# One pool of five PSUM banks for the first products of two MLPs, on one Trainium2 core

## Chip, cores and metric

The kernel runs on one core of one Trainium2 chip. The metric is the device time of one execution in microseconds (us), as the median of several runs. Instructions are named with the line of the kernel that issues them (L683), and engines by short names: PE is TensorE (matmuls), PEld its weight loads, DVE is VectorE, ACT is ScalarE, POOL is GpSimd, SP issues most of the DMAs.

## What is computed

A long convolution (a Hyena filter) of 12480 tokens with 128 channels, gated by x, goes through two MLPs of 2048 inner features each, the first with an ELU, the second with a leaky ReLU of one slope per feature:

```python
h_filt = (np.maximum(pos_emb @ w1, 0.0) @ w2) * np.exp(-0.01 * pos)[:, None]
Uf = np.fft.rfft(x * v, n=2 * S, axis=1)
Hf = np.fft.rfft(h_filt, n=2 * S, axis=0)
x = x * np.fft.irfft(Uf * Hf, n=2 * S, axis=1)[:, :S]

h = x @ w_in                                   # first MLP, 128 -> 2048
g = np.where(h > 0.0, h, np.exp(np.minimum(h, 0.0)) - 1.0)
x = g @ w_out                                  # 2048 -> 128
h = x @ w_in2                                  # second MLP
g = np.maximum(h, 0.0) + alpha * np.minimum(h, 0.0)
out = g @ w_out2
```

## The kernel before

Up to some 280 us the kernel does the filter, the Fourier transforms (as matmuls) and the product of the spectra. The rest of the time belongs to the MLPs, and the change lies in them.

**Tiles and steps.** The tokens are cut into 26 tiles of columns: one of 392, twelve of 490, twelve of 485 (run as 486) and one of 388. Channels or features lie on the partitions. Each MLP takes a tile in 16 chunks of 128 features, so there are 416 steps, s = 16 t + c. In each step a chunk's first product h = x @ w_in is made in one PSUM bank, the activation is applied to it, and the second product adds it to the tile's output, which stays in a bank of its own for 16 steps. The second MLP runs 23 steps (`RAMP`) behind the first, since it needs the first one's finished tile: steps 0 to 22 are the first MLP's alone, then both run, and the last 23 steps are the second one's alone.

**Precision.** All operands are pairs of a rounded float32r value and its rest, `h` and `l` in the names. A product is therefore three matmuls (`mm3`, lines 638, 639 and 640): high x high, then high weights x low data, then low weights x high data. A step of both MLPs has four products, twelve matmuls on PE in this order: the first product of MLP 1 (tile `psh`, from `x1h`, `x1l`), the first product of MLP 2 (`psh`, from `x2h`, `x2l`), the second product of MLP 1 of three steps before (`pso`, from `g1h`, `g1l`), and that of MLP 2 (`pso`, from `g2h`, `g2l`).

**The activations.** For MLP 1, ACT makes exp(min(h, 0)) in two passes over the bank (L675, L676), or in one while MLP 1 is alone (L673, with a minimum on DVE at L682); DVE then takes the maximum with h (L683), which is the last reading of that bank. For MLP 2 all is on DVE: L701 (min, times alpha) and L706 (max, plus), the last reading of its bank. ACT rounds the result to the high half (L689 for `g1h`, L712 for `g2h`), and the low half is a subtraction (L661, `g1l` and `g2l`): one in four on DVE, the others on POOL, in other steps for the one MLP than for the other.

**The order.** The instructions of each engine stand in the order in which the loop at the end of the program writes them; no scheduler moves them. On DVE a step is: L701 and L706 of MLP 2, the low half of MLP 2 and that of MLP 1 of the step before (in the steps that are DVE's), and last L683 of MLP 1. An instruction that reuses a buffer waits for the last reader of what was in it.

**Other work beside the MLPs.** Once per tile the inverse transform (`inv2`, L539, 20 to 24 small matmuls into tile `psi`, read by DVE at L541) makes the next tile's input. From step 54 to 154 every fifth step has the transform of four high residues (`high_mm`): three matmuls of 512 columns, which DVE copies out (L587). In steps 10, 14, 18 and 22 there is a shorter one of a single matmul (L584), copied out by ACT.

**The eight PSUM banks** in the MLPs: two for `psi`, which `inv2` and `high_mm` share; two (`psh1`) for the first products of MLP 1 and two (`psh2`) for those of MLP 2; one each for the two outputs (`pso1`, `pso2`). While one MLP is alone, its first products take the four `psh` banks in turn (`tset`). So, while both run, the first product of MLP 1 in step s takes the bank that L683 of step s-2 has read last:

```python
    def tset(s, mlp):
        alone = s < RAMP if mlp == 1 else s >= NT * NFF - RAMP
        return 3 - mlp if alone and s % 2 else mlp
```

Of the kernel before, what the change touches and what calls it, by code (L numbers as in the profile page):

```python
# [9 lines left out]
F32 = mybir.dt.float32  # L10
# [4 lines left out]
PSUM = bass.MemoryType.PSUM  # L15
# [31 lines left out]
def kernel(ctx: ExitStack, tc: tile.TileContext, posT, w1b, w2b, sc2, xva, xT,  # L47
# [4 lines left out]
    def pool(name, bufs=1, **kw):  # L52
        return tc.tile_pool(name=name, bufs=bufs, reuse_waits="tile", **kw)
# [20 lines left out]
    def col(o, n):  # L74
        return ureg[:, o : o + n]
# [503 lines left out]
    def high_mm(i):  # L579
        y, n = hst.pop(i)  # L580
        z = col(512 * i if i < NFILL else 1024 + 512 * (i % 2), n * D)
        ps = pst.tile([128, 512], F32, name="psi")
        if i < NFILL:
            nc.tensor.matmul(ps[:, : n * D], w_sb, y, start=True, stop=True)  # L584
        else:
            mm3(ps, n * D, wf, yf, True, True)
        (nc.scalar.copy if i < NFILL else nc.vector.tensor_copy)(z.rearrange("q (f h c) -> q f h c", f=n, h=NCH),  # L587
                                                                 ps[:, : n * D].rearrange("q (h f c) -> q f h c", f=n, h=NCH))
        nc.sync.dma_start(zd[4 * i : 4 * i + n].rearrange("f q c -> q f c"), z.rearrange("q (f c) -> q f c", f=n))
# [28 lines left out]
    take(ctx.enter_context(pool("wp2")), "wi2l", "wo2h", "wo2l")  # L618
    gp = ctx.enter_context(pool("gp", 2, side="right"))
    pp.close()  # L620
    pst = ctx.enter_context(pool("pst", 2, space=PSUM))
    psm = ctx.enter_context(pool("psm", 2, space=PSUM))

    LAG = 3
    LAG_ALONE = 5
# [9 lines left out]
    def mm3(ps, w, a, b, start, stop):  # L635
        ah, al = a
        bh, bl = b
        nc.tensor.matmul(ps[:, :w], ah, bh[:, :w], start=start, stop=False)  # L638
        nc.tensor.matmul(ps[:, :w], ah, bl[:, :w], start=False, stop=False)  # L639
        nc.tensor.matmul(ps[:, :w], al, bh[:, :w], start=False, stop=stop)  # L640

    def wc(nm, c):
        return (wh[nm][0][:, c, :], wh[nm][1][:, c, :])
# [4 lines that stand above are left out]
# [4 lines left out]
    def h1_mm(s):  # L652
        t, c = divmod(s, NFF)
        hi, lo, w = x1[t]
        ps = psm.tile([128, 512], F32, name=f"psh{tset(s, 1)}")
        mm3(ps, w, wc("wi1", c), (hi, lo), True, True)
        st1[s] = [ps, w]

# [78 lines left out]
    def h2_mm(s):  # L737
        t, c = divmod(s, NFF)
        hi, lo, w = x2[t]
        ps = psm.tile([128, 512], F32, name=f"psh{tset(s, 2)}")  # L740
        mm3(ps, w, wc("wi2", c), (hi, lo), True, True)
        st2[s] = [ps, w]

# [29 lines left out]
    for i, x in enumerate(FILL):  # L773
        at(x, high_mm, i)
    for i in range(NFILL, (NF + 3) // 4):
        for d, fn in ((-1, high_load), (1, high_add), (2, high_split), (4, high_mm)):
            at(HS + 5 * i + d, fn, i)
# [10 lines left out]
    for s in range(-1, TOT + RAMP + LAG_ALONE + 1):  # L788
        if s >= 0:
            if s < TOT:  # L790
                h1_mm(s)
            s2 = s - RAMP
            if 0 <= s2 < TOT:
                h2_mm(s2)
# [129 lines left out]
```

## Time and profile before

| | us |
|---|---|
| median of 3 runs | 1480.73 (1479.01 to 1482.35) |
| span of the profiled execution, first to last instruction | 1475.1 |
| median less span | 5.6 |
| PE busy | 1415.1 (96%) |
| DVE busy | 1280.5 (87%) |
| ACT busy | 1076.3 (73%) |
| POOL busy | 1019.4 (69%) |

The page gives no other time of the profiled execution than its span. What lies around the span, before the first and after the last instruction, is taken from the median of the runs. Busy times are unions of the intervals that the profiler gives. A matmul is listed from its start to its modelled end, and the next one starts before that end, so PE's busy time isn't its time at its peak: distances from start to start tell more. In a list of waits, a row says which engine's instruction (line and tile) sat idle for which instruction of another engine: the sum in us, how often, and the longest. A weight load waits first where a matmul waits, since it stands right ahead of it.

### The profile page before, as it was taken

To read this page: it belongs to the slowest core of one execution; us is meant where nothing else is said; L and a number is where in the kernel's file an instruction comes from. 1 tells how busy PE (TensorE), PEld (TensorE's weight loads), DVE (VectorE), ACT (ScalarE), POOL (GpSimd) and SP (SyncE) were. 2 spreads that over 40 slices of the span, in tenths; PEclk is the share of its full clock that TensorE was granted. 3 is DMA by queue.
4 is the path that set the end of the run, shared out by engine and by line. 5 is a ranking of instruction groups with operands and counts; after the bars stand their busy time and mean duration, and the time that the engine had idled before them with its cause. 6 is when DMAs were issued, how large, how long until landed. Compare 5 with 4: busy or idle time off the path is not lost.

```text
span 1475.1 us, 26820 instructions
## 1 busy us (share of the span) xinstructions
PE 1415.1 (96%) x9935; PEld 1200.8 (81%) x9935; DVE 1280.5 (87%) x1812; ACT 1076.3 (73%) x2009; POOL 1019.4 (69%) x935
## 2 busy tenths in 40 slices
PE   7988778899999999999999999999999999999998
PEld 6878676888888878888888888888888888888887
DVE  5689986798888888888889999998999899889998
ACT  3445442478877787788878788888888787888884
POOL 4668975456778887888756676666666666766667
PEclk9999999999999999999999999999999999999999
DMA  8786898540131212212003200000000000000000
GB/s 258 235 267 174 225 276 210 197 132 18 38 89 51 89 60 68 89 51 78 31 25 127 82 18 26 25 25 25 8 18 25 25 25 8 18 25 22 7 8 13
DMA packets 70215, 117.64 MB, mean 80 GB/s; under 512 B 8806, under 2 KB 41258, under 8 KB 68920
## 3 DMA queue, kind: packets, MB, share of 16 engines
q1 hardware_dynamic: 65716, 104.49, 23.2%
q0 software_dynamic: 1296, 7.86, 1.6%
q10 hardware_dynamic: 3072, 3.57, 0.7%
q8 instruction: 78, 1.28, 0.4%
q14 instruction: 53, 0.43, 0.1%
HBM read 82.38 MB, written 32.80 MB: 78 GB/s over the span
## 4 chain that ended last, share of the span: by engine, by line
PE 64%; DVE 9%; ACT 5%; issue 3%; POOL 1%; DMA 1%; SPq 0%; POOLq 0%; ACTq 0%; DVEq 0%
PE psh L638 11%; PE psh L640 10%; PE psh L639 10%; PE pso L639 10%; PE pso L638 10%; PE pso L640 10%; PE psi L539 3%; DVE ureg L683 2%; DVE g1l L661 1%; DVE ureg L701 1%; ACT ureg L676 1%; DVE g2l L661 1%; ACT ureg L675 1%; DVE ureg L706 1%; ACT g2h L712 1%
## 5 line engine op out<-in xcount | busy, mean ns | idle before, releaser
L661 POOL TENSOR_TENSOR g2l<-ureg,g2h 128x490 fp32r<-128x490 f32 (+3 forms) x315 | 373.1, 1185 | 131.7 <-ACT g2h L712 62.4
L661 POOL TENSOR_TENSOR g1l<-ureg,g1h 128x486 fp32r<-128x486 f32 (+3 forms) x313 | 346.6, 1108 | 164.2 <-ACT g1h L689 160.8
L701 DVE TENSOR_SCALAR ureg<-psh,al_sb 128x486 f32<-128x486 f32 (+3 forms) x416 | 295.9, 711 | 80.0 <-PE psh L640 75.7
L675 ACT ACTIVATE ureg<-psh 128x490 f32<-128x490 f32 (+2 forms) x393 | 225.5, 574 | 112.9 <-PE psh L640 97.3
L706 DVE SCALAR_TENSOR_TENSOR ureg<-psh,ureg 128x486 f32<-128x486 f32 (+3 forms) x416 | 274.1, 659 | 14.3
L683 DVE SCALAR_TENSOR_TENSOR ureg<-ureg,psh 128x486 f32<-128x486 f32 (+3 forms) x416 | 268.2, 645 | 4.5 <-ACT ureg L676 3.2
L689 ACT CAST g1h<-ureg 128x490 fp32r<-128x490 f32 (+3 forms) x405 | 240.3, 593 | 16.0 <-DVE ureg L683 13.5
L676 ACT ACTIVATE ureg<-ureg 128x490 f32<-128x490 f32 (+2 forms) x393 | 239.7, 610 | 12.4
L712 ACT CAST g2h<-ureg 128x490 fp32r<-128x490 f32 (+3 forms) x404 | 234.6, 581 | 8.4 <-DVE ureg L706 6.8
L638 PE MATMUL psh<-x1h,wi1h 128*128 128x486 f32 (+3 forms) x416 | 170.2, 409 | 9.4 <-DVE ureg L683 6.9
L639 PE MATMUL psh<-x1l,wi1h 128*128 128x486 f32 (+3 forms) x416 | 158.7, 382 | 0.0
L640 PE MATMUL psh<-x1h,wi1l 128*128 128x486 f32 (+3 forms) x416 | 158.7, 381 | 0.0
L638 PE MATMUL psh<-x2h,wi2h 128*128 128x486 f32 (+3 forms) x416 | 158.7, 381 | 0.0
L639 PE MATMUL psh<-x2l,wi2h 128*128 128x486 f32 (+3 forms) x416 | 158.6, 381 | 0.0
L640 PE MATMUL psh<-x2h,wi2l 128*128 128x486 f32 (+3 forms) x416 | 158.3, 381 | 0.0
L638 PE MATMUL pso<-g1h,wo1h 128*128 128x490 f32 (+3 forms) x405 | 154.8, 382 | 1.5 <-ACT ureg L731 1.5
L639 PE MATMUL pso<-g2l,wo2h 128*128 128x490 f32 (+3 forms) x404 | 154.3, 382 | 0.7 <-POOL g2l L661 0.7
L640 PE MATMUL pso<-g1h,wo1l 128*128 128x490 f32 (+3 forms) x405 | 154.8, 382 | 0.0
L639 PE MATMUL pso<-g1l,wo1h 128*128 128x490 f32 (+3 forms) x405 | 154.6, 382 | 0.0
L640 PE MATMUL pso<-g2h,wo2l 128*128 128x490 f32 (+3 forms) x404 | 154.0, 381 | 0.0
L638 PE MATMUL pso<-g2h,wo2h 128*128 128x490 f32 (+3 forms) x404 | 153.8, 381 | 0.0
L661 DVE TENSOR_TENSOR g1l<-ureg,g1h 128x490 fp32r<-128x490 f32 (+3 forms) x104 | 124.7, 1199 | 19.3 <-ACT g1h L689 8.8
(167 smaller groups left out, 2531.9 us busy)
## 6 DMA issues: line engine op xcount, KB each, us to landing
ureg<-yd SPq DMA_DIRECT2D x50, 256.0 KB
yd<-rreg SPq DMA_DIRECT2D x22, 512.0 KB
rreg<-in_gmat_dram SPq DMA_DIRECT2D x24, 384.0 KB
ureg<-in_finv_dram SPq DMA_DIRECT2D x23, 379.0 KB
ureg<-zd SPq DMA_DIRECT2D x4, 1584.0 KB
x<-in_xva_dram SPq DMA_DIRECT2D x32, 196.0 KB
v<-in_xva_dram SPq DMA_DIRECT2D x32, 196.0 KB
zd<-ureg SPq DMA_DIRECT2D x24, 256.0 KB
```

The costliest lines, as they stand in the source:

```text
L539: nc.tensor.matmul(ps[w_, a * ni : (a + 1) * ni], z_sb[:, c * P + p0 + a, w_], fv[:, a, c, :ni], start=(c == 0), stop=(c == 1))
L638: nc.tensor.matmul(ps[:, :w], ah, bh[:, :w], start=start, stop=False)
L639: nc.tensor.matmul(ps[:, :w], ah, bl[:, :w], start=False, stop=False)
L640: nc.tensor.matmul(ps[:, :w], al, bh[:, :w], start=False, stop=stop)
L661: eng.tensor_tensor(lo[:, :w], e[:, :w], hi[:, :w], ALU.subtract)
L675: nc.scalar.activation(e[:, :w], ps[:, :w], AF.Relu, scale=-1.0)
L676: nc.scalar.activation(e[:, :w], e[:, :w], AF.Exp, scale=-1.0)
L683: nc.vector.scalar_tensor_tensor(e[:, :w], e[:, :w], -1.0, ps[:, :w], op0=ALU.add, op1=ALU.max)
L689: nc.scalar.copy(hi[:, :w], e[:, :w])
L701: nc.vector.tensor_scalar(e[:, :w], ps[:, :w], 0.0, al_sb[:, c : c + 1], op0=ALU.min, op1=ALU.mult)
L706: nc.vector.scalar_tensor_tensor(e[:, :w], ps[:, :w], 0.0, e[:, :w], op0=ALU.max, op1=ALU.add)
L712: nc.scalar.copy(hi[:, :w], e[:, :w])
```

## The change

The pool `pst` has one bank instead of two, for the inverse transform alone. The pool `psm` has five banks under one name, `psh`, beside the two for the outputs. The first products of both MLPs and the high residues' transform take their bank from those five, through `h_bank`. `tset` stays for the buffers in SBUF.

```diff
@@ high_mm
-        ps = pst.tile([128, 512], F32, name="psi")
+        ps = h_bank()
@@ pools
-    pst = ctx.enter_context(pool("pst", 2, space=PSUM))
-    psm = ctx.enter_context(pool("psm", 2, space=PSUM))
+    pst = ctx.enter_context(pool("pst", 1, space=PSUM))
+    psm = ctx.enter_context(pool("psm", 5, space=PSUM))
+
+    def h_bank():
+        return psm.tile([128, 512], F32, name="psh")
@@ h1_mm
-        ps = psm.tile([128, 512], F32, name=f"psh{tset(s, 1)}")
+        ps = h_bank()
@@ h2_mm
-        ps = psm.tile([128, 512], F32, name=f"psh{tset(s, 2)}")
+        ps = h_bank()
```

Each engine has the same instructions in the same order as before (lines behind 621 are numbered three higher). What differs are the banks and the waits. The pool hands out the bank that was let go longest ago, in the order of the program. In a step of both MLPs, where L706 stands ahead of L683, the first product of MLP 1 gets the bank that L683 of step s-3 read last, and the first product of MLP 2 the one that L706 of step s-2 read last. Behind a `high_mm`, for two steps, MLP 1 gets a bank let go by L706 of step s-2 and MLP 2 one let go by L683 of step s-2.

On PE, one step of both MLPs in the long stretch behind the high residues (x1h, x1l and x2h, x2l are the two MLPs' inputs, wi1, wi2 and wo1, wo2 the weights; DVE_49 is DVE's semaphore, Pool_49 POOL's, Activation_49 ACT's). Before:

```order
L638 MATMUL psh1_9269<-x1h_9100,wi1h_2996 128x486 [waits DVE_49]
L639 MATMUL psh1_9269<-x1l_9101,wi1h_2996 128x486
L640 MATMUL psh1_9269<-x1h_9100,wi1l_2997 128x486
L638 MATMUL psh2_9273<-x2h_8850,wi2h_3000 128x490
L639 MATMUL psh2_9273<-x2l_8851,wi2h_3000 128x490
L640 MATMUL psh2_9273<-x2h_8850,wi2l_3228 128x490
L638 MATMUL pso1_8879<-g1h_9225,wo1h_2998 128x490 [waits Activation_49]
```

And with the change:

```order
L641 MATMUL psh_9269<-x1h_9100,wi1h_2996 128x486 [waits DVE_49]
L642 MATMUL psh_9269<-x1l_9101,wi1h_2996 128x486
L643 MATMUL psh_9269<-x1h_9100,wi1l_2997 128x486
L641 MATMUL psh_9273<-x2h_8850,wi2h_3000 128x490 [waits DVE_49]
L642 MATMUL psh_9273<-x2l_8851,wi2h_3000 128x490
L643 MATMUL psh_9273<-x2h_8850,wi2l_3228 128x490
L641 MATMUL pso1_8879<-g1h_9225,wo1h_2998 128x490 [waits Activation_49]
```

The banks of the two MLPs are of one pool now, and the first product of MLP 2 has a wait for DVE of its own; before, the wait of the product ahead of it covered it.

On PE, behind a transform of high residues (tile read: yh, yl; weights: wh, wl), before:

```order
L638 MATMUL psi_5309<-yh_3244,wh_3242 128x512 [waits PE_49,Activation_49]
L639 MATMUL psi_5309<-yl_3245,wh_3242 128x512 [waits Pool_49]
L640 MATMUL psi_5309<-yh_3244,wl_3243 128x512
L638 MATMUL psh1_5317<-x1h_5159,wi1h_2996 128x490 [waits DVE_49]
L639 MATMUL psh1_5317<-x1l_5160,wi1h_2996 128x490
L640 MATMUL psh1_5317<-x1h_5159,wi1l_2997 128x490
L638 MATMUL psh2_5321<-x2h_4895,wi2h_3000 128x490
```

And with the change:

```order
L641 MATMUL psh_5309<-yh_3244,wh_3242 128x512 [waits DVE_49,Activation_49]
L642 MATMUL psh_5309<-yl_3245,wh_3242 128x512 [waits Pool_49]
L643 MATMUL psh_5309<-yh_3244,wl_3243 128x512
L641 MATMUL psh_5317<-x1h_5159,wi1h_2996 128x490 [waits DVE_49]
L642 MATMUL psh_5317<-x1l_5160,wi1h_2996 128x490
L643 MATMUL psh_5317<-x1h_5159,wi1l_2997 128x490
L641 MATMUL psh_5321<-x2h_4895,wi2h_3000 128x490 [waits DVE_49]
```

The transform's product takes one of the five banks and waits for DVE to have let go of it, where it waited for a bank of `psi`.

## Rows read from the trace of the kernel before

**Rows 1.** The page: span, busy time by engine, the chain that ended last.

```profile
span 1475.1 us, 26820 instructions
...
PE 1415.1 (96%) x9935; PEld 1200.8 (81%) x9935; DVE 1280.5 (87%) x1812; ACT 1076.3 (73%) x2009; POOL 1019.4 (69%) x935
...
PE 64%; DVE 9%; ACT 5%; issue 3%; POOL 1%; DMA 1%; SPq 0%; POOLq 0%; ACTq 0%; DVEq 0%
```

**Rows 2.** Windows: stretch, its us, busy PE, PEld, DVE, ACT, POOL, granted clock, DMA.

```profile
500.00:600.00 100.00, 98.13 (x497) 81.21 (x496) 85.90 (x126) 80.19 (x149) 81.58 (x67) 1.00 0.22 66
1000.00:1100.00 100.00, 99.61 (x507) 82.75 (x506) 90.11 (x128) 82.32 (x153) 66.36 (x60) 1.00 0.06 19
```

**Rows 3.** Waits of weight loads, 280:315, 315:402, 402:690, 690:1400, 1400:1475: us, times, longest.

```profile
PEld psh L638 <- DVE ureg L683: 5.1, 3, 3.3
...
PEld psh L638 <- DVE ureg L683: 5.0, 9, 1.5
...
PEld psh L638 <- DVE ureg L683: 6.7, 15, 1.0
...
PEld psh L638 <- DVE ureg L683: 19.6, 49, 0.6
...
PEld psh L638 <- DVE ureg L683: 1.2, 4, 0.4
```

**Rows 4.** Timeline, 900 to 906 us: start, duration, engine, instruction [idle before].

```profile
900.27 0.67 DVE L706 SCALAR_TENSOR_TENSOR ureg<-psh,ureg 128x490 f32<-128x490 f32 x1
...
901.87 0.65 DVE L683 SCALAR_TENSOR_TENSOR ureg<-ureg,psh 128x486 f32<-128x486 f32 x1
...
902.28 0.39 PE L640 MATMUL pso<-g2h,wo2l 128*128 128x490 f32 x1
...
902.57 0.19 PEld L638 LDWEIGHTS psh<-x1h,wi1h 128*128 128x128 f32 x1 [0.33 <-DVE ureg L683]
902.58 0.49 PE L638 MATMUL psh<-x1h,wi1h 128*128 128x486 f32 x1
...
902.90 0.38 PE L639 MATMUL psh<-x1l,wi1h 128*128 128x486 f32 x1
...
903.34 0.39 PE L638 MATMUL psh<-x2h,wi2h 128*128 128x490 f32 x1
...
905.12 0.39 PE L640 MATMUL pso<-g2h,wo2l 128*128 128x490 f32 x1
905.12 0.19 PEld L638 LDWEIGHTS psh<-x1h,wi1h 128*128 128x128 f32 x1
...
905.34 0.38 PE L638 MATMUL psh<-x1h,wi1h 128*128 128x486 f32 x1
```

**Rows 5.** Timeline of the first steps of the MLPs, around 288 and 320 us.

```profile
288.30 0.50 ACT L673 ACTIVATE ureg<-psh 128x392 f32<-128x392 f32 x1 [3.42 <-POOL ureg L571]
...
319.02 0.49 PE L638 MATMUL psh<-x1h,wi1h 128*128 128x490 f32 x1 [1.13 <-DVE ureg L683]
...
320.00 0.58 ACT L675 ACTIVATE ureg<-psh 128x490 f32<-128x490 f32 x1
```

**Rows 6.** Waits of DVE, 315:402, 402:690 and 690:1400 us.

```profile
DVE ureg L701 <- PE psh L640: 5.9, 11, 0.8
...
DVE ureg L701 <- PE psh L640: 20.9, 34, 1.0
...
DVE ureg L701 <- PE psh L640: 46.8, 87, 0.8
```

**Rows 7.** Timeline, 569 to 571 us.

```profile
569.47 1.06 POOL L661 TENSOR_TENSOR g1l<-ureg,g1h 128x490 fp32r<-128x490 f32 x1
...
570.61 0.46 PE L639 MATMUL pso<-g1l,wo1h 128*128 128x490 f32 x1
```

**Rows 8.** Tiles g1l and g2l, DVE's part: count, ns min/median/max, first and last start.

```profile
L661 DVE TENSOR_TENSOR g1l<-ureg,g1h x104: 557/1305/1506, 290.2 to 1434.5; 128x490 fp32r<-128x490 f32 x48, 128x486 fp32r<-128x486 f32 x48, 128x392 fp32r<-128x392 f32 x4, 128x388 fp32r<-128x388 f32 x4
...
L661 DVE TENSOR_TENSOR g2l<-ureg,g2h x100: 654/1138/1739, 327.5 to 1450.8; 128x490 fp32r<-128x490 f32 x48, 128x486 fp32r<-128x486 f32 x48, 128x392 fp32r<-128x392 f32 x4
```

## The prediction

> **What bounds the kernel now.** The page comes first: in a span of 1475.1 us TensorE is busy 96%, and the chain that ended last lies 64% on it [rows 1]. Then the busy time by stretches: between 500 and 600 us PE is busy 98.13 of 100 us, between 1000 and 1100 us 99.61, at a granted clock of 1.00 (its higher level) in both [rows 2]. Those numbers hide what is lost, because a matmul's modelled end overlaps the next start. What counts is the distance from start to start.
>
> The timeline shows it [rows 4]. Undisturbed, matmuls of 486 to 490 columns follow at 0.22 us: 905.12 to 905.34, with the weights of 905.34 loaded from 905.12 on. At 902.58 this breaks. The first product of the first MLP (L638, psh from x1h) needs a PSUM bank that DVE's L683 of two steps before has just let go: L683 starts at 901.87 and takes 0.65, so it ends at 902.52, and the weight load goes at 902.57 after 0.33 us of idleness. From 902.28 to 902.90 lie two distances, 0.62 instead of 0.44: 0.18 us are lost. So **a stall costs PE its listed weight-load wait less 0.15 us** (0.33 against 0.18).
>
> The waits of the weight loads by stretch [rows 3] give the sum of what this bank wait takes, at that 0.15 per stall:
> - 280 to 315 us (first MLP alone): 5.1 − 3 x 0.15 = 4.65
> - 315 to 402: 5.0 − 9 x 0.15 = 3.65
> - 402 to 690 (the high residues are done here): 6.7 − 15 x 0.15 = 4.45
> - 690 to 1400: 19.6 − 49 x 0.15 = 12.25
> - 1400 to the end: 1.2 − 4 x 0.15 = 0.6
>
> Together 25.6 us, 1.7% of the time. Is the next engine close behind? DVE waits for PE's products (L701 for L640) 5.9, 20.9 and 46.8 us in the three middle stretches [rows 6], 73.6 us in all, against 20.35 us lost by PE in the same ones. DVE is the nearest rival, but has 3.6 times what it needs.
>
> **The change part by part.** No instruction is added, removed or put elsewhere; only banks, and with them waits, change.
>
> *First product of the first MLP.* With two banks of its own it waits for L683 of step s−2, the last thing that DVE does in that step. From five banks, handed out in the order in which they were let go, it gets one that L683 of step s−3 released. In the stall shown, that bank was free a whole step earlier (a step is twelve distances of 0.22, 2.7 us), while the longest wait in 690 to 1400 us is 0.6. So this wait goes.
>
> *First product of the second MLP.* It now carries a wait of its own, for L706 of step s−2; behind it on PE stand eight more products of the step; DVE's L701 needs the first two of them, and the next step's products, which ACT's L675 needs, queue behind all eight. In the timeline that L706 ends at 900.94 and the product starts at 903.34 [rows 4], 2.4 us later: never late. A wait that is already fulfilled could still break the pulling ahead of weights; the row at 905.34 says no, since that product carried such a wait too and lost nothing. I take 0; the other end, the 0.10 of the late second distance (902.58 to 902.90 instead of 0.22) times 393, is excluded by that row.
>
> *The high residues' transform* takes one of the five banks every fifth step, and DVE's copy gives it back in the same step. In the two steps behind it the banks shift: the first MLP gets one released by L706, the second MLP one released by L683 of two steps before. That is the old wait, but three products (0.66 us) further on. The longest wait in 402 to 690 us is 1.0, a loss of 0.85, so at most some 0.2 of one stall is left. In the ramp ACT gives that bank back; it is let go about as early as DVE's. Nothing.
>
> *One bank for the inverse transform.* It is used once in 16 steps, over 40 us apart, and its reader follows within the step: 0.
>
> *What of the 25.6 is on the path.* 280 to 315: PE waits, but so does everyone: ACT starts its second exponential at 288.30 after 3.42 us of waiting for POOL [rows 5], and the ramp then runs at the pace of ACT and DVE. Taken 0, bounds 0 and 4.65. 315 to 402: the longest wait, 1.5 us before 319.02, stands in front of an ACT that starts the next L675 only at 320.00 [rows 5], so I count half of its 1.35: 3.65 − 0.7 = 2.95, bounds 2.3 (without that wait) and 3.65. 402 to 690: 4.45 less some 0.45 for the shifted banks and tight low halves (first rival) = 4.0, bounds 2.2 (half) and 4.45. 690 to 1400: 12.25 in full, since DVE has 46.8 us to spare there; the lower bound is 8.2, two thirds, as if every third stall only changed its cause. Behind 1400 DVE paces the end: 0, bounds 0 and 0.6. **Sum 2.95 + 4.0 + 12.25 = 19.2 us**, bounds 12.7 and 25.6.
>
> The profile gives the span, 1475.1; the median of the three runs, 1480.7, is 5.6 more, which lies around the span and doesn't change. So the span should be 1455.9, and the time **1461.5 us**.
>
> **The rivals.**
> - *Half the gain.* With PE earlier by up to 0.4 us, the next thing to be late is POOL's low half of g1, which the second product's L639 needs. For it: at 570.61 that product starts 0.08 us after POOL's 569.47 + 1.06 [rows 7], and POOL is busy 81.58 of 100 us in that stretch. Against it: POOL is busy only 66.36 in the longest one [rows 2]. If it gave back the 4.0 of 402 to 690 and half of the 12.25, 9.1 would remain: 1471.6.
> - *No change.* The loss only moves, because the end is set by DVE's total, and PE's stalls merely show it; or the pool hands the first MLP a bank of step s−2 as before. Against both: DVE's 73.6 us of waiting, and the order in which five banks come round. 1480.7.
> - *Slower: DVE's low halves stretch.* A quarter of the low halves of either MLP run on DVE, 104 and 100 of them, and one of g2 takes anything from 0.65 to 1.74 us; the medians are 1.31 and 1.14 [rows 8]. If PE's new rhythm laid each of them over a POOL operation, DVE would become the bound. The point from which this decides: the 73.6 us of slack spread over 204 operations are 0.36 us each, so their mean has to rise from about 1.2 to over 1.56 before anything is lost against now. At 1.6 it costs 0.4 x 204 − 73.6 = 8 us: 1488.7. It would take nearly the longest of them as the rule, so it is unlikely. The Trainium skill has the mechanism: "SBUF — State Buffer", section "Who interferes with whom", says that a DVE instruction with two SBUF inputs contends with a GpSimd instruction that reads SBUF. The trace agrees so far as one takes up to 2.7 times the shortest, at widths that differ by a quarter; how often the two would meet after the change it can't show.
>
> **How the numbers follow.** Forecast 0.78, half the gain 0.12, no change 0.06, slower 0.04. A measurement of this kernel can tell about 0.2%, 3 us, from no change. The first two are faster: 0.90; same 0.06; slower 0.04. The range runs from 1457 (nearly the whole 25.6) to 1470, past the lower bound of my sum (1480.7 − 12.7 = 1468.0) and up to the half-gain case; what lies outside is the better end of the ramp, that rival and the two below it, about 2 in 10.
>
> **What would show each step right or wrong.** Right: in 690 to 1400 us the weight loads' waits for DVE's release of psh fall from 49 to a handful, the first product is followed after 0.22 everywhere, DVE's wait for L640 shrinks by 10 to 15 us, and the stretch becomes 12 us shorter. The ramp up to 315 us keeps its length within 2 us. Half the gain: L639 on pso waits for POOL's g1l in dozens of places. Slower: DVE's L661 has a median near 1.6 and L701 no longer waits for PE. I am wrong if the bank waits are gone and the span isn't shorter by at least 11 us, or if the second MLP's product now waits.

## The result

The changed kernel takes 1459.24 us (median of 4 runs, 1457.69 to 1460.95), the kernel before beside it 1480.81 (4 runs, 1479.01 to 1482.35): a ratio of 0.9855, 95% interval 0.9841 to 0.9869. It is faster by 21.6 us. Forecast were 1461.5 and a range of 1457 to 1470. Medians and ratios in this text are of fast runs: one run of 7820 us (e1_third_mlp1) and one of 2286 us (r_after, at a granted clock of 0.556) are left out.

In the changed kernel the lines lie three further down: L641, L642 and L643 are the matmuls L638, L639 and L640, L686 is DVE's L683, L704 its L701, L664 the low halves of L661.

The page after, its span, busy times and chain, beside [rows 1]:

```profile
span 1458.0 us, 26810 instructions
...
PE 1401.9 (96%) x9935; PEld 1208.7 (83%) x9935; DVE 1278.4 (88%) x1812; ACT 1073.8 (74%) x2009; POOL 1019.6 (70%) x935
...
PE 77%; DVE 2%; DMA 1%; POOL 1%; issue 0%; ACT 0%; SPq 0%; POOLq 0%; DVEq 0%; ACTq 0%
```

PE's share of the span is 96% before and after, and says nothing. The chain does: 64% of it lay on PE, 9% on DVE and 5% on ACT; now it is 77, 2 and 0%. The windows after (stretch, its us, busy PE, PEld, DVE, ACT, POOL, granted clock, DMA), beside [rows 2]:

```profile
500.00:600.00 100.00, 98.36 (x503) 82.66 (x502) 87.06 (x127) 80.42 (x148) 84.16 (x69) 1.00 0.21 66
...
1000.00:1100.00 100.00, 100.00 (x517) 85.25 (x516) 91.93 (x130) 82.90 (x154) 66.91 (x61) 1.00 0.06 19
```

Between 1000 and 1100 us PE starts 517 matmuls where it started 507, and DVE is busier in the same 100 us because the same work comes in less time. The weight loads' waits after, in 402 to 687 and 687 to 1383 us (steps 54 to 150 and 150 to 400, as 402 to 690 and 690 to 1400 before), all of them, beside [rows 3]:

```profile
PEld psi L539 <- issue: 2.1, 6, 0.3
PEld pso L641 <- ACT ureg L734: 2.0, 1, 2.0
PEld pso L642 <- POOL g1l L664: 0.6, 3, 0.2
PEld pso L641 <- ACT ureg L758: 0.5, 1, 0.5
...
PEld psi L539 <- issue: 4.1, 12, 0.4
PEld psi L539 <- PE pso L642: 1.4, 4, 0.3
```

No weight load waits for DVE's release of a `psh` bank any more: 15 and 49 waits are 0 and 0, and nothing of their kind stands in their place (POOL's g1l: 3 waits, 0.6 us; the 2.0 us for L734 stood there before as 1.9 us for L731). The timeline shows it at the step of [rows 4], which now lies at 895:

```profile
891.65 0.65 DVE L686 SCALAR_TENSOR_TENSOR ureg<-ureg,psh 128x486 f32<-128x486 f32 x1
...
894.59 0.65 DVE L686 SCALAR_TENSOR_TENSOR ureg<-ureg,psh 128x486 f32<-128x486 f32 x1
...
894.97 0.39 PE L643 MATMUL pso<-g2h,wo2l 128*128 128x490 f32 x1
894.98 0.19 PEld L641 LDWEIGHTS psh<-x1h,wi1h 128*128 128x128 f32 x1
...
895.20 0.38 PE L641 MATMUL psh<-x1h,wi1h 128*128 128x486 f32 x1
895.20 0.19 PEld L642 LDWEIGHTS psh<-x1l,wi1h 128*128 128x128 f32 x1
895.41 0.39 PE L642 MATMUL psh<-x1l,wi1h 128*128 128x486 f32 x1
```

DVE is no earlier against PE than it was: its L686 of two steps before runs from 894.59 to 895.24. But the product takes the bank that the L686 before that one let go at 892.30, 2.9 us earlier, so its weights are pulled ahead at 894.98 while the late L686 still runs, and the matmuls follow at 0.23, 0.21.

What PE no longer waits for, DVE no longer has to spare. Its waits after, in 319 to 402, 402 to 687 and 687 to 1383 us, beside [rows 6]:

```profile
DVE ureg L704 <- PE psh L643: 2.6, 6, 0.7
...
DVE ureg L704 <- PE psh L643: 14.7, 29, 0.9
...
DVE ureg L704 <- PE psh L643: 34.7, 86, 0.8
```

They went from 73.6 to 52.0 us, 21.6 less. To place the gain I cut the MLPs by the starts of the first MLP's 416 first products, the last part ending with the last matmul:

| steps | before, us | after | gain | taken in the prediction |
|---|---|---|---|---|
| 0 to 23 | 32.68 | 33.69 | −1.01 | 0 |
| 23 to 54 | 86.21 | 82.43 | 3.78 | 2.95 |
| 54 to 150 | 288.94 | 285.12 | 3.82 | 4.0 |
| 150 to 400 | 709.18 | 696.35 | 12.83 | 12.25 |
| 400 to the last matmul | 71.82 | 71.33 | 0.50 | 0 |
| together | 1188.83 | 1168.92 | 19.9 | 19.2 |

### The profile page after: what moved, and what is told of

It reads as the page before. It is cut to its first block, busy times and chain, and to the rows that moved or that the text cites. A ratio compares the mean times of both kernels' runs of the same rounds, so it can differ in the third digit from the quotient of the medians.

```text
span 1458.0 us, 26810 instructions
## 1 busy us (share of the span) xinstructions
PE 1401.9 (96%) x9935; PEld 1208.7 (83%) x9935; DVE 1278.4 (88%) x1812; ACT 1073.8 (74%) x2009; POOL 1019.6 (70%) x935
## 4 chain that ended last, share of the span: by engine, by line
PE 77%; DVE 2%; DMA 1%; POOL 1%; issue 0%; ACT 0%; SPq 0%; POOLq 0%; DVEq 0%; ACTq 0%
PE psh L641 13%; PE psh L642 12%; PE psh L643 12%; PE pso L642 12%; PE pso L643 12%; PE pso L641 12%; PE psi L539 3%; DMA ureg<-yd 1%; DMA spreg<-in_wo_dram 0%; DVE ureg L704 0%; POOL ureg L571 0%; PE psh L584 0%; DVE wo1l L139 0%; DVE ureg L709 0%; SPq L402 0%
## 5 line engine op out<-in xcount | busy, mean ns | idle before, releaser
L664 POOL TENSOR_TENSOR g1l<-ureg,g1h 128x486 fp32r<-128x486 f32 (+3 forms) x313 | 346.6, 1107 | 163.3 <-ACT g1h L692 160.1
L664 POOL TENSOR_TENSOR g2l<-ureg,g2h 128x490 fp32r<-128x490 f32 (+3 forms) x315 | 373.5, 1186 | 110.5 <-ACT g2h L715 43.0
L704 DVE TENSOR_SCALAR ureg<-psh,al_sb 128x486 f32<-128x486 f32 (+3 forms) x416 | 295.9, 711 | 56.7 <-PE psh L643 53.4
L709 DVE SCALAR_TENSOR_TENSOR ureg<-psh,ureg 128x486 f32<-128x486 f32 (+3 forms) x416 | 274.1, 659 | 14.3
L686 DVE SCALAR_TENSOR_TENSOR ureg<-ureg,psh 128x486 f32<-128x486 f32 (+3 forms) x416 | 268.3, 645 | 4.7 <-ACT ureg L679 3.7
L641 PE MATMUL psh<-x1h,wi1h 128*128 128x486 f32 (+3 forms) x416 | 162.6, 391 | 3.6 <-DVE ureg L686 2.6
L643 PE MATMUL psh<-x1h,wi1l 128*128 128x486 f32 (+3 forms) x416 | 158.7, 381 | 0.0
L642 PE MATMUL psh<-x1l,wi1h 128*128 128x486 f32 (+3 forms) x416 | 158.5, 381 | 0.0
L641 PE MATMUL psh<-x2h,wi2h 128*128 128x486 f32 (+3 forms) x416 | 158.5, 381 | 0.0
L642 PE MATMUL psh<-x2l,wi2h 128*128 128x486 f32 (+3 forms) x416 | 158.4, 381 | 0.0
L643 PE MATMUL psh<-x2h,wi2l 128*128 128x486 f32 (+3 forms) x416 | 158.2, 380 | 0.0
L641 PE MATMUL pso<-g1h,wo1h 128*128 128x490 f32 (+3 forms) x405 | 155.1, 383 | 3.1 <-ACT ureg L734 1.6
L642 PE MATMUL pso<-g1l,wo1h 128*128 128x490 f32 (+3 forms) x405 | 155.0, 383 | 0.0
L643 PE MATMUL pso<-g1h,wo1l 128*128 128x490 f32 (+3 forms) x405 | 154.9, 383 | 0.0
L642 PE MATMUL pso<-g2l,wo2h 128*128 128x490 f32 (+3 forms) x404 | 154.3, 382 | 0.6 <-POOL g2l L664 0.6
L641 PE MATMUL pso<-g2h,wo2h 128*128 128x490 f32 (+3 forms) x404 | 154.0, 381 | 0.1
L643 PE MATMUL pso<-g2h,wo2l 128*128 128x490 f32 (+3 forms) x404 | 153.9, 381 | 0.0
L664 DVE TENSOR_TENSOR g1l<-ureg,g1h 128x490 fp32r<-128x490 f32 (+3 forms) x104 | 126.2, 1213 | 22.1 <-ACT g1h L692 11.5
```

Source lines behind the costliest of these rows:

```text
L664: eng.tensor_tensor(lo[:, :w], e[:, :w], hi[:, :w], ALU.subtract)
L686: nc.vector.scalar_tensor_tensor(e[:, :w], e[:, :w], -1.0, ps[:, :w], op0=ALU.add, op1=ALU.max)
L704: nc.vector.tensor_scalar(e[:, :w], ps[:, :w], 0.0, al_sb[:, c : c + 1], op0=ALU.min, op1=ALU.mult)
L709: nc.vector.scalar_tensor_tensor(e[:, :w], ps[:, :w], 0.0, e[:, :w], op0=ALU.max, op1=ALU.add)
```

## The experiments

Three questions were open: which of the three parts of the change brings the gain (the sharing, the fifth bank, or the place of the high residues); why DVE let the bank go late at all; and whether DVE is really far from being the bound, as the last rival doubted. Each kernel's ratio, with its 95% interval, is to runs of the kernel before on the same chip: their median was 1479.09 us for e1, e2, e3 and e5, 1478.08 for e4, e6, e7 and e8, and 1481.29 for the last four.

**e1_third_mlp1.** The banks stay apart: three for the first MLP, two for the second, one for `psi`, which the inverse transform and the high residues share. From before:

```diff
-    pst = ctx.enter_context(pool("pst", 2, space=PSUM))
+    pst = ctx.enter_context(pool("pst", 1, space=PSUM))
+    def h_bank(m):
+        return psm.tile([128, 512], F32, name=f"psh{m}", bufs=(None, 3, 2)[m])
-        ps = psm.tile([128, 512], F32, name=f"psh{tset(s, 1)}")
+        ps = h_bank(tset(s, 1))
-        ps = psm.tile([128, 512], F32, name=f"psh{tset(s, 2)}")
+        ps = h_bank(tset(s, 2))
```

> Banks stay split: three for the first products of MLP 1, two for MLP 2, one for the inverse transform and the high residues together. The theory (PE lost time only where MLP 1's first product waited for L683 of two steps before): with a third bank it waits for L683 of step s-3, so the whole gain is here without any sharing: 1457 to 1463 us, no wait of a weight load for L683 between steps 54 and 400. Rival 'sharing' (it is the common pool that helps, because either MLP can take any free bank): 1475 to 1481. Rival 'the transform needs its second bank': 1465 or more, with waits of PE on psi between 400 and 690 us.

Measured: 1464.73 us, ratio 0.9892 (0.9845 to 0.9939), slower than the 1457 to 1463 expected. The theory holds for the bank: from step 54 on no weight load waits for L686, without any sharing. What it left out is the rival of the transform's second bank. What is lost against the change lies in two places, where the high residues' matmuls stand behind the inverse transform in one step, and in the granted clock behind them (last section); weight loads from 305 to 1400 us:

```profile
PEld psi L641 <- DVE ureg L541: 4.2, 2, 2.2
```

**e2_four_shared.** Both MLPs share the four `psh` banks that there were, and `psi` keeps its two; so no bank more, only another order of use:

```diff
-    psm = ctx.enter_context(pool("psm", 2, space=PSUM))
+    psm = ctx.enter_context(pool("psm", 4, space=PSUM))
+    def h_bank():
+        return psm.tile([128, 512], F32, name="psh")
```

and `h_bank()` in both first products, as in the change.

> Four banks in one pool for both first products, two for the transforms as before: no bank more than before, only another order of use. MLP 1 now takes a bank let go by L706 of step s-2, MLP 2 one let go by L683 of step s-2, three matmuls (0.66 us) further on. The theory: the stalls of 690 to 1400 us were at most 0.4 us long (wait 0.6 less 0.15), so nearly all vanish: 1459 to 1464 us. Rival 'count' (five banks instead of four are what helps): 1477 to 1482, with as many waits as before, now at the first product of MLP 2.

Measured: 1459.34 us, 0.9871 (0.9842 to 0.9901), the changed kernel's time. Steps 150 to 400 take 696.35 us, the same to the last digit. Of the waits for L686 two are left, both before step 150 and both at the first product of the second MLP:

```profile
PEld psh L641 <- DVE ureg L686: 0.7, 2, 0.4
```

So **the order in which banks come round makes the gain of the change, and the fifth bank none of it.** (A third bank for the first MLP alone, in e1_third_mlp1, ends the same waits another way.) With two banks each, the bank that the first MLP takes is always the one that the last, late L686 of two steps before let go. With four in turn it takes one that L709 let go, earlier in DVE's step, and the second MLP, three matmuls later on PE, takes the late one.

**e3_third_mlp2.** The third bank goes to the second MLP instead: `bufs=(None, 2, 3)[m]` in the edit of e1_third_mlp1, nothing else.

> Banks split the other way: two for MLP 1 as before, three for MLP 2, one for the transforms. The theory: MLP 1's wait is untouched, so 1478 to 1482 us and again some 64 waits of weight loads for L683 between steps 54 and 400. Rival 'count' (five first-product banks, wherever): 1458 to 1465.

Measured: 1481.66 us, 1.0018 (0.9998 to 1.0038). A bank more in the wrong place brings nothing; the waits of before are nearly all there (305 to 1400 us):

```profile
PEld psh L641 <- DVE ureg L686: 29.7, 70, 1.0
...
PEld psi L641 <- DVE ureg L541: 2.7, 2, 1.7
```

**e4_high_psi.** The change without its third part: the high residues stay in the one `psi` bank. From after:

```diff
-        ps = h_bank()
+        ps = pst.tile([128, 512], F32, name="psi")
```

in `high_mm`.

> The change without its third part: five banks in one pool for the first products, but the high residues' transform goes to the one bank of the inverse transform. The first experiment of this study left two waits of PE there (high residues for L541, 4.2 us in two), with a granted clock of 0.98 in the two stretches they fall in. The theory: in the two steps (74 and 154) in which both transforms stand, PE waits some 2 us for DVE's L541, and the clock falls behind it: 1462 to 1467 us, 3 to 7 us behind the change. Rival (that run was slower for its split banks, three and two): 1458 to 1461, and no such loss.

Measured: 1463.36 us, 0.9897 (0.9874 to 0.9919). The same two waits as in e1_third_mlp1, of steps 74 and 154, which take 7.49 and 7.09 us instead of 5.41 and 5.24 in a second profile of the changed kernel (r_after): 3.9 us together. That much the third part of the change saves at those steps, once `psi` has one bank. The ratio lies 0.42%, some 6 us, above that of the change (0.9897 against 0.9855, and the intervals don't meet), so the two steps need not be all of it. The other half of the expectation did not come in this profile: the granted clock stayed at 1.00 behind both waits (last section).

**e5_apart.** Why is L683 late? The timeline of DVE before, ahead of the stall of [rows 4], shows it:

```profile
896.11 0.73 DVE L701 TENSOR_SCALAR ureg<-psh,al_sb 128x490 f32<-128x490 f32 x1 [0.75 <-POOL g2l L661]
...
897.67 1.35 DVE L661 TENSOR_TENSOR g1l<-ureg,g1h 128x486 fp32r<-128x486 f32 x1
898.95 0.65 DVE L683 SCALAR_TENSOR_TENSOR ureg<-ureg,psh 128x486 f32<-128x486 f32 x1
...
900.86 1.09 DVE L661 TENSOR_TENSOR g2l<-ureg,g2h 128x490 fp32r<-128x490 f32 x1
...
903.78 0.65 DVE L683 SCALAR_TENSOR_TENSOR ureg<-ureg,psh 128x486 f32<-128x486 f32 x1
...
905.69 0.65 DVE L683 SCALAR_TENSOR_TENSOR ureg<-ureg,psh 128x486 f32<-128x486 f32 x1
...
906.95 0.73 DVE L701 TENSOR_SCALAR ureg<-psh,al_sb 128x490 f32<-128x490 f32 x1 [0.61 <-PE psh L640]
```

A step of DVE without a low half takes 1.91 us (903.78 to 905.69), one with a low half about 3 (898.95 to 901.87, the L683 of [rows 4]), and PE's step 2.7. Two long ones come in succession, so DVE falls behind, and then waits for PE. The edit, with the banks of before, moves the low halves of the second MLP that are DVE's by one step:

```diff
-        lo_part(s + 2, hi, lo, e, w, s > TOT - NFF)
+        lo_part(s + 1, hi, lo, e, w, s > TOT - NFF)
```

> The kernel before, with its banks, but DVE's low halves of the two MLPs lie two steps apart instead of in neighbouring steps (the low half of MLP 2 falls on DVE one step later in the count). The theory says that L683 is late only in the second of two long DVE steps that follow each other (2.0 us of work besides, 1.2 us per low half, against a PE step of 2.7): spread out, each long step is caught up in the next, and the stalls vanish without a bank: 1459 to 1466 us. Rival 'two banks are too few by themselves' (latency of matmul, ACT and DVE, not the backlog): 1476 to 1482.

Measured: 1461.50 us, 0.9884 (0.9855 to 0.9913), most of the gain of the change with no bank touched. Its DVE between the same kind of steps:

```profile
897.91 0.66 DVE L661 TENSOR_TENSOR g2l<-ureg,g2h 128x490 fp32r<-128x490 f32 x1
898.48 0.66 DVE L683 SCALAR_TENSOR_TENSOR ureg<-ureg,psh 128x486 f32<-128x486 f32 x1
...
900.56 0.65 DVE L683 SCALAR_TENSOR_TENSOR ureg<-ureg,psh 128x486 f32<-128x486 f32 x1
...
903.50 1.10 DVE L661 TENSOR_TENSOR g1l<-ureg,g1h 128x486 fp32r<-128x486 f32 x1 [0.26 <-ACT g1h L689]
```

Long and short steps alternate. Left of the waits (305 to 1400 us):

```profile
PEld psh L638 <- DVE ureg L683: 4.5, 9, 1.1
```

There was a second effect: DVE's g2 halves themselves became short.

```profile
L661 DVE TENSOR_TENSOR g2l<-ureg,g2h x98: 556/666/1680, 336.1 to 1425.0; 128x490 fp32r<-128x490 f32 x48, 128x486 fp32r<-128x486 f32 x46, 128x392 fp32r<-128x392 f32 x4
```

The median is 666 ns instead of 1138 [rows 8]. The length goes with the moment at which a half starts. In the kernel before, 194 of DVE's 204 halves started while a POOL instruction was running, and 185 of them ended 0.515 to 0.535 us behind that instruction's end; the other ten took at most 671 ns. The g2 half at 900.86 above is one of the 185: it ends at 901.95, and beside it ran

```profile
900.38 1.05 POOL L661 TENSOR_TENSOR g1l<-ureg,g1h 128x486 fp32r<-128x486 f32 x1 [1.87 <-ACT g1h L689]
```

to 901.43, 0.52 us earlier. With the edit only 32 of the 98 g2 halves start while POOL is at work, and the other 66 take at most 671 ns. The Trainium skill says in "SBUF — State Buffer", section "Who interferes with whom", that a DVE instruction with two SBUF inputs contends with a GpSimd instruction that reads SBUF; these counts agree with it.

So the edit did two things at once, and this run doesn't part them: it set the halves apart, and it made most of the second MLP's short. Eleven g2 halves between 305 and 1400 us still took over 1.1 us, and five of the nine waits left stand behind one of them. That spacing alone would be enough is not shown.

**e6_apart_after.** The edit of e5_apart on top of the change.

> The change, and DVE's low halves two steps apart as well. The theory says that both cure the same wait, so nothing is left for the second one: 1457 to 1462 us. Rival (DVE's backlog costs something else besides, or the changed rhythm against POOL does): off by over 3 us either way.

Measured: 1456.97 us, 0.9853 (0.9825 to 0.988), at the lower edge of what was expected. Steps 150 to 400 take 696.67, no less than the change alone. In steps 54 to 150 the stretch is 282.77 instead of 285.12: the wait of 2.0 us for ACT's L734 (the second line of the waits after) is 0.2 there. At a change of tiles ACT copies the old output out before PE may start the next one, and here ACT comes to it nearly in time. That the even steps are the reason is not shown: e4_high_psi and r_six, without them, have 1.1 and 0.9 us there.

**e7_six.** All six banks in one pool, the inverse transform's among them. From after:

```diff
-        ps = ps_tile() if t < 2 else pst.tile([128, 512], F32, name="psi")
+        ps = ps_tile() if t < 2 else h_bank()
-    pst = ctx.enter_context(pool("pst", 1, space=PSUM))
-    psm = ctx.enter_context(pool("psm", 5, space=PSUM))
+    psm = ctx.enter_context(pool("psm", 6, space=PSUM))
```

> No bank for the inverse transform alone: six banks in turn for both first products and both transforms. The theory: no wait for a bank was left on PE between steps 54 and 400, so a sixth bank brings nothing there: 1456 to 1461 us. Rival (more banks, more gain): below 1455.

Measured: 1454.03 us, 0.9838 (0.9813 to 0.9863), below the range expected and in the rival's. But steps 150 to 400 take 696.35 again: a sixth bank brings nothing there. The profile names the release of a bank by DVE ahead of 15 of the inverse transform's weight loads, 5.2 us in all; yet the gaps ahead of these loads are 24, of 8.2 us together, here and in the changed kernel, where they have other names, so no wait was added. The lower total came largely from steps 0 to 23 (29.42 us against 33.69), which the last four kernels take up.

**e8_dve_third.** Is DVE near to being the bound? The change with the low halves apart, and one in three of them on DVE instead of one in four (136 and 136 instead of 104 and 100):

```diff
-        eng = nc.vector if s % 4 == 0 and not last else nc.gpsimd
+        eng = nc.vector if s % 3 == 0 and not last else nc.gpsimd
-        lo_part(s + 2, hi, lo, e, w, s > TOT - NFF)
+        lo_part(s + 1, hi, lo, e, w, s > TOT - NFF)
```

> The change, with one low half in three on DVE instead of one in four, 70 operations of 1.2 us more on DVE, 84 us. It measures the room that DVE has left. With the change DVE still waits for PE some 2, 15 and 35 us in the three stretches, 52 in all. If that is room, the time grows by what goes beyond it: 84 - 52 = 32, 1480 to 1500 us, and DVE's wait for L643 is nearly gone. Rival (DVE has far more room than its waits show, since POOL's relief counts too): under 1465. Rival (DVE sets the end already): 1535 or more.

Measured: 1464.86 us, 0.9904 (0.988 to 0.9929). I had expected 1480 to 1500, and missed; the time lies just inside the rival with more room (under 1465). The window from 400 to 1384 us, in this kernel:

```profile
400.00:1384.00 984.00, 983.94 (x5109) 834.58 (x5109) 930.65 (x1319) 815.37 (x1499) 624.28 (x562) 1.00 0.13 43
```

and in e6_apart_after, which differs from it by the share alone:

```profile
400.00:1384.00 984.00, 983.98 (x5111) 834.91 (x5110) 861.71 (x1261) 809.13 (x1500) 715.16 (x619) 1.00 0.13 43
```

DVE has 68.9 us more to do (71.7 in the whole span, where I had put 84), and still is busy only 930.65 of 984, while PE has no gap left. So the price was about right; the room was not. The expectation took DVE's wait for L643 as the room, 52 us of the changed kernel, where DVE is busy 894.39 us in this window. The kernel that gets the further halves, e6_apart_after, has 122 us without work on DVE there, since its g2 halves are short, and 53 are left with them. Steps 150 to 400 take 696.49 against 696.67. What it costs lies ahead: against e6_apart_after, 7.9 us faster by the medians on the same chip, its profile is 5.0 us longer, of it 2.1 in the ramp and 2.3 in steps 23 to 54; from 285 to 402 us L686 is waited for 7 times, 4.0 us, in e6_apart_after 3 times, 1.3 us. So even a third more low halves on DVE don't make it the bound once both MLPs run steadily, with the halves apart.

**r_after, r_apart, r_six, e9_six_apart.** The last four ran together, to see whether a version beats the change: the change itself, the two from above, and both edits at once (e9_six_apart: the edits of e7_six and of e5_apart on after).

> The changed kernel itself once more, beside the three versions that follow, so that they stand on one chip. Theory: about 1459 us (1457 to 1462), with the stretch from step 150 to step 400 at 696.3 us. Rival (that the totals of the versions differ only by the chip of the job): all four kernels of this job lie within 0.2% (3 us) of each other.

> The change with VectorE's low halves apart once more. Theory: about 2 us below the changed kernel (1457), all of it from the step at the tile change near step 99, where PE waits for ScalarE's copy into the output no longer; from step 150 to 400 nothing is to be had, since PE already runs without a gap there (696.3 us). Rival: no difference over 1 us.

> Six banks in one pool, the inverse transform's among them, once more. Theory: 1 to 2 us below the changed kernel (1457 to 1458), since its bank is one more that a late VectorE can hold; the stretch from 150 to 400 the same 696.3. Rival: the 1454.0 of the earlier job was its ramp (29.4 us for the first 23 steps) and the total is the changed kernel's within 1 us here.

> Six banks in one pool and VectorE's low halves apart. Theory: 1455 to 1457, the smaller of the two before, since both leave only the same stretch of PE's own work (696.3 from step 150 to 400) and the same tail; the gain over the changed kernel is that of steps 0 to 150 alone, some 3 us. Rival: nothing beyond either of the two, or the changed kernel's time within 1 us.

| kernel | median, us | ratio to before | 0 to 23 | 54 to 150 | 150 to 400 |
|---|---|---|---|---|---|
| r_after | 1458.05 | 0.9848 (0.9825 to 0.9871) | 28.61 | 284.86 | 696.35 |
| r_apart | 1459.56 | 0.9851 (0.9828 to 0.9875) | 28.85 | 282.78 | 696.67 |
| r_six | 1457.25 | 0.9851 (0.9825 to 0.9876) | 28.48 | 283.67 | 696.35 |
| e9_six_apart | 1457.07 | 0.9840 (0.9818 to 0.9862) | 29.09 | 282.78 | 696.61 |

The rival of r_after holds: they lie within 2.5 us, and all four intervals overlap. The 2 us in steps 54 to 150 are there again in the profiles, but too small for the totals: r_apart was expected 2 us below r_after and lies 1.5 above. And e7_six's 1454.0 is not shown to be the sixth bank: the same kernel, r_six, takes 1457.25, and in the profiles the MLPs take 1164.06 us in e7_six and 1164.15 in r_after. No version is shown to beat the change: from step 150 to 400 all have PE without a gap, at 696.35 us or three tenths more.

## Why the prediction was right, and where not

*What bounds the kernel, and the price of a stall.* Right. 49 waits of 19.6 us in steps 150 to 400 gave 12.83 us back, so on average a stall costs its wait less 0.14 us ((19.6 − 12.83) / 49); I had taken 0.15 from one place.

*First product of the first MLP.* Right: from step 23 to 400 the bank of three steps before was always free in time. e1_third_mlp1 and e3_third_mlp2 show that this product alone had the wait.

*First product of the second MLP at 0.* Right: the full list of waits after has none on it. e2_four_shared shows even the tighter case, in which it takes the late bank itself.

*High residues in the pool, one bank for the inverse transform at 0.* Right, and only together: e4_high_psi has the one bank without the move, and pays 3.9 us at two steps. The prediction had counted both at nothing without seeing that the second rests on the first.

*What of the 25.6 is on the path.* 402 to 690 came to 3.82 of my 4.0; 690 to 1400 to 12.83 of 12.25. In 315 to 402 I had counted half of the longest wait, since ACT stood close behind, and the stretch gave 3.78, more than the whole sum of its stalls (3.65), or 3.20 by the profile of r_after: that half was too careful by 0.2 to 0.8 us. Behind 1400 I took 0, for DVE pacing the end; it gave 0.50 of the bound 0.6. That step was wrong, by half a microsecond. Together the last four gained 20.9 where I had 19.2, or 20.6 by the profile of r_after.

*The ramp at 0.* It cost 1.01 us in this profile. But in a second profile of the same kernel it took 28.61 us instead of 33.69, so a comparison of one execution each says nothing on it (the last section shows where the 5 us lie). The gain from it, if any, stays open, and with such a spread it is partly luck that the time came within 2.3 us of the forecast.

*Median less span.* **This step failed.** I put the 5.6 us between the median of before and the span of its profiled execution down to what lies around the span. Around it lie 1.8 us: 1459.77 less 1458.0 in the profile after, and 1.7 to 1.9 in every run of either kernel that lists its span. So by the same 1.8 the profiled execution of before took some 1476.9 us (an estimate), nearly 4 below its median. In it the MLPs started at 282.88 us, in the profile after at 285.67, though the part ahead of them is the same program; in the other twelve profiles they start between 285.06 and 289.90. The forecast hardly suffered, as the sum was taken from the median in the end, but whoever compares the two spans reads 17.1 us of gain where the medians give 21.6 and the MLPs' stretches 19.9.

*The rivals.* Half the gain: POOL's g1l is waited for 3 times instead of in dozens of places. No change: the gain itself excludes it, and e2_four_shared against e3_third_mlp2 shows that the order in which the banks come round makes it. Slower through DVE: its low halves kept their lengths (g1l and g2l after, beside [rows 8]):

```profile
L664 DVE TENSOR_TENSOR g1l<-ureg,g1h x104: 557/1308/1514, 293.6 to 1417.5; 128x490 fp32r<-128x490 f32 x48, 128x486 fp32r<-128x486 f32 x48, 128x392 fp32r<-128x392 f32 x4, 128x388 fp32r<-128x388 f32 x4
...
L664 DVE TENSOR_TENSOR g2l<-ureg,g2h x100: 655/1140/1577, 330.3 to 1433.7; 128x490 fp32r<-128x490 f32 x48, 128x486 fp32r<-128x486 f32 x48, 128x392 fp32r<-128x392 f32 x4
```

Its point of decision, 73.6 us more on DVE, was not reached: e8_dve_third has 36.3 us more of DVE's work between 400 and 1384 us than the changed kernel (930.65 against 894.39), half of that, and from step 54 on it pays next to nothing for it. Where a loss would begin stays open.

## To carry to other kernels

A bank wait asks three things: which instruction lets the bank go, where in its engine's step that one stands, and who takes the bank next. Here sharing two pairs of banks in turn gave the whole gain with no bank more, and a bank more for the wrong product gave none; setting apart the long steps of the engine that lets go, which also shortened them, did most of it. The size of the gain could be read ahead here from the weight loads' waits, less 0.14 us each, since the next engine had more waiting than that in the same stretch; and a single profiled execution should be set against the median before its span is compared with another.

## What was unexpected of the hardware

The granted clock can fall after a gap of PE that leaves it alone another time. In e1_third_mlp1 and in e4_high_psi PE waits the same 1.77 us at step 154. PE's timeline in e1_third_mlp1:

```profile
708.15 0.44 PE L641 MATMUL psi<-yh,wh 128*128 128x384 f32 x1 [1.77 <-DVE ureg L541]
...
709.39 0.61 PE L643 MATMUL psh<-x1h,wi1l 128*128 128x490 f32 x1
709.80 0.61 PE L641 MATMUL psh<-x2h,wi2h 128*128 128x490 f32 x1
...
712.55 0.38 PE L642 MATMUL pso<-g2l,wo2h 128*128 128x490 f32 x1
```

and in e4_high_psi:

```profile
703.40 0.44 PE L641 MATMUL psi<-yh,wh 128*128 128x384 f32 x1 [1.77 <-DVE ureg L541]
...
704.48 0.38 PE L643 MATMUL psh<-x1h,wi1l 128*128 128x490 f32 x1
704.70 0.39 PE L641 MATMUL psh<-x2h,wi2h 128*128 128x490 f32 x1
```

In the first the distances are 0.41 us until 712.25, the granted clock from 708 to 712 us is 0.62, partly at the lower level (1.2 GHz), and the step behind takes 4.21 us instead of 2.68; in the second they stay at 0.22 and the clock at 1.00. The same 1.5 us lie behind the wait of step 74 (the next step takes 4.23 us instead of 2.69). So of e1_third_mlp1's loss against e4_high_psi in these two profiles some 3 us are clock, not waiting.

In the ramp of the changed kernel a low clock stands behind a longer wait. Its window from 290 to 300 us in the profile after, and then in r_after:

```profile
290.00:300.00 10.00, 7.32 (x24) 6.59 (x25) 8.67 (x17) 5.90 (x13) 7.09 (x8) 0.66 0.10 20
```

```profile
290.00:300.00 10.00, 9.13 (x43) 6.88 (x41) 9.72 (x19) 7.24 (x16) 6.67 (x8) 1.00 0.24 73
```

The same program ran 24 matmuls in one and 43 in the other, at a clock of 0.66 and 1.00, after PE had been busy 17.58 and 19.20 of the 20 us before. The two ramps differ by 5 us, more than any term of my sum but one. But the difference begins ahead of the clock. In the profile after:

```profile
287.70 3.95 POOL L571 TENSOR_TENSOR ureg<-ureg 128x512 f32<-128x512 f32 x3 [3.12 <-DMA ureg<-yd]
289.00 0.50 ACT L676 ACTIVATE ureg<-psh 128x392 f32<-128x392 f32 x1 [2.60 <-POOL ureg L571]
291.17 0.44 PE L641 MATMUL psh<-x1h,wi1h 128*128 128x392 f32 x1 [2.58 <-DVE ureg L686]
...
293.43 0.70 PE L641 MATMUL pso<-g1h,wo1h 128*128 128x392 f32 x1 [1.46 <-ACT g1h L692]
...
297.28 0.53 PE L642 MATMUL psh<-x1l,wi1h 128*128 128x392 f32 x1
```

and the same wait for L686 in r_after:

```profile
290.93 0.45 PE L641 MATMUL psh<-x1h,wi1h 128*128 128x392 f32 x1 [0.32 <-DVE ureg L686]
```

In the first POOL waits for a transfer (`ureg<-yd`), ACT's exponential for POOL, DVE for ACT and PE for DVE: L676 waits 4.8 us for L571 in all, in r_after not at all. PE's waits for other engines are 4.0 us there against 0.9. Behind them, from 294.17 to 299.24, PE's matmuls follow at about 0.33 us instead of 0.18, which costs some 2.4 us (an estimate: 15 distances, 5.07 us instead of 2.7). So by these figures the larger part of the 5 us is a transfer that came late against the MLPs' start, and the clock the smaller. Why the clock falls behind one gap and not behind another stays open.
